# Decode attention with a gated MLP on one Trainium2 core: value products, queries and one projection take other places in the order of work

## The chip, the cores and the metric

The kernel runs on one core of one Trainium2 chip. The metric is device time in microseconds of one execution, the median of several runs. Beside the times there is one profiled execution, whose trace gives every instruction's start and duration and every DMA's issue.

## The reference, cut to what matters

Four sequences decode one token each. There are 32 heads of 128, a cache of 4096 keys and values per head, a model width of 512 and a gated MLP of 1792. All inputs are bf16.

```python
mod = (silu(c) @ w_mod).reshape(4, 6, 1, 512)          # sa, ca, ga, sb, cb, gb
h = layernorm(x) * (1 + ca) + sa
q = (h @ wq).reshape(4, 1, 32, 128)
p = softmax(q @ k_cache^T / sqrt(128))                 # 4 x 32 x 4096
x = x + ga * ((p @ v_cache).reshape(4, 1, 4096) @ wo)
h = layernorm(x) * (1 + cb) + sb
z = gelu(h @ w_in); z1, z2 = halves of z; z2 = layernorm(z2)
x = x + gb * ((z1 * (w_sp * z2 + b_sp)) @ w_out)
```

Keys and values are 134 MB each; all inputs together are 283 MB, and each byte is read once.

## The kernel before, in words

**Tiles.** The loop at L697 runs over 32 key tiles `i` of four heads each, 128 partitions by 128 key positions by 128 (4.2 MB). Tiles 0 to 23 come in pairs (`i` and `i + 1`): eight heads of one batch in one load of 8.4 MB. Tiles 24 to 31 are single. Keys alternate between the buffers bufA and bufB. Values use bufC, which a pair fills wholly and a single tile half; the values of tiles 30 and 31 go to bufB. `L` is 31.

**One tile.** VectorE multiplies the keys by the query in place, in two halves (`mult`, L391). TensorE sums the products over the head's width by matmuls with an identity (`reduce_d`, L399; 16 matmuls for a whole half, 4 for a quarter of one). VectorE sums what is left of that (`sum8`, L422), and three quarters of the second half by itself (`sum_rest`, L411). After a pair, or a single tile, `scores` takes the maxima (L435 to L452) and ScalarE the exponentials (`exps`, L465). `norm_r`, `norm_a` and `norm_b` (L479 to L502) sum them and invert. `pv` (L517) multiplies the exponentials by the values, 64 matmuls for a pair and 32 for a single tile; its result stands in `opss[0]` or `opss[1]` until `o_pick` (L526, L530), `o_cols` (L539, L542) and `o_scale` (L564, L570) have turned it into columns of the head outputs.

**Queries.** `queries(n)` for n from 0 to 7 does one batch and one half of the heads; with n = 0 and n = 4 come 16 matmuls with `wq` (L317), which lies in bufC. Each then spreads its rows by two or three matmuls into one PSUM tile (`qps`) that ScalarE copies out (L334, L335). `queries(0)` stands ahead of the loop, the others inside tile 0: two ahead of `mult(0, 1)`, five after `reduce_d(0, 1)`. `late_mod_a` (L352) and `late_mod_b` (L362 to L372, in tile 0) make the modulation of the later part.

**Output projection.** The heads of tiles 0 to 23 form three groups of eight. `deal(k)` (L636) and `dealt(k)` (L648, L654) bring a group's outputs into the layout of `wo`, and `project` (L666) multiplies all 24 heads in 24 matmuls; its result is copied out at L670. `turn` (L677, L681) adds the heads of tiles 24 to 27 and turns the rows into columns; `o_proj` (L611) does tiles 28 to 31. `add_up` (L688) adds the parts. Behind these come the second layer norm, the MLP (`gate`, L883; L908) and one product with `w_mod` (L916).

**Order.** Each engine works its instructions in the order in which the program issues them: the kernel switches to manual scheduling, and nothing is reordered. Semaphores order the engines among each other. All large loads are issued on SyncE's queue: `load_k`, `load_v`, `load_wo`, `load_end`. Each issue waits until its buffer is free, with all later ones behind it. In a pair's odd tile the value load is issued after the value product of the pair before, and at the tile's end the key load three tiles ahead.

**Where the value products stand.** In an odd tile `i` up to 23, `pv(i - 2)` follows `reduce_d(i, 0)`. For the later ones there are tables:

```python
PV_MID = {25: 23, 27: 24, 29: 26}     # after reduce_d(i, 0)
PV_END = {27: 25, 29: 27, 31: 28}     # at the end of tile i
```

`pv(29)` and `pv(30)` are called behind the loop.

**The end.** `deal(0)` and `deal(1)` run in tile 30, `deal(2)` and `deal(3)` at the end of tile 31; `dealt(0)` in tile 30, `dealt(1)` in tile 31 and the others behind the loop. There follow `project`, the steps of tile 28's output, `turn`, `pv(29)` with its steps, and `pv(30)` with its own.

Of the kernel before, what the change touches and what calls it, by code (L numbers as in the profile page):

```python
# [20 lines left out]
KIN = (slice(0, 2), slice(2, 4))  # L21
KG = (slice(0, 3), slice(3, 4))

PV_MID = {25: 23, 27: 24, 29: 26}
PV_END = {27: 25, 29: 27, 31: 28}
PICKS = {28: (24, 25), 30: (26, 27)}


# [25 lines left out]
def kernel(  # L54
# [16 lines left out]
    nc = tc.nc  # L71
    P = 128
    B, _, D = A_x.shape
# [83 lines left out]
    def load_v(i):  # L157
        if i < N0:
            load(bufC, kv_view(A_v_cache, i), (NP,))
        else:  # L160
            load(vts[i], kv_view(A_v_cache, i), TAIL if i == L else (NJ,))
# [148 lines left out]
    def queries(n):  # L310
        h, b = divmod(n, B)
        gs = slice(h * GQ, (h + 1) * GQ)
        if b == 0:
            qr = ps_sm([P, GQ, DH])
            for k in range(DJ):
                for q in range(HQ):
                    nc.tensor.matmul(  # L317
                        qr[R * q:R * (q + 1)], lhsT=hT[:, k, :], rhs=wq_v[:, k, gs, q, :],
                        start=(k == 0), stop=(k == DJ - 1), tile_position=(0, R * q),
                    )  # L320
            nc.scalar.copy(out=qrow[:, h], in_=qr)
        qp = ps_q().rearrange("p (g d) -> p g d", g=GQ)
        npair = 2 - h
        for k in range(2):
            nc.tensor.matmul(
                qp[:, 0:npair], lhsT=eb2[k][:, b].rearrange("p k q r -> p (k q r)"),
                rhs=qrow[:, h, k:2 * npair:2], start=(k == 0), stop=(k == 1),
            )
        if h:
            nc.tensor.matmul(  # L330
                qp[:, 2:4], lhsT=eb[:, b].rearrange("p q r -> p (q r)"), rhs=qrow[:, h, 2:4],
                start=True, stop=True,
            )
            nc.scalar.copy(out=qbo[:, :, b, :], in_=qp[:, 2:4])  # L334
        nc.scalar.copy(out=qbp[:, 2 * h:2 * h + npair, b, :], in_=qp[:, 0:npair])  # L335

    queries(0)

    sp_t = pre.tile([1, 2], BF16, name="sp_t")
    nc.scalar.dma_start(out=sp_t[:, 0:1], in_=B_w_sp[0:1, 0:1])  # L340
# [52 lines left out]
    def reduce_d(i, kc):  # L393
        ns = on_pe(i, kc)
        rd = 512 // ns
        kt = kts[i][:, kc * KC:kc * KC + ns, :]
        red = ps_red().rearrange("p (n r) -> p n r", r=rd)
        for m in range(DH // rd):
            nc.tensor.matmul(  # L399
                red, lhsT=ident_bf, rhs=kt[:, :, m * rd:(m + 1) * rd],  # L400
                start=(m == 0), stop=(m == DH // rd - 1),
            )
        st[i, "red", kc] = red
# [83 lines left out]
    def norm_a(i):  # L487
        if not pair(i):
            rsb = st.pop((i, "rsb"))
        elif i % (2 * B) == 2 * B - 1:  # L490
            rsb = st.pop(("P", i // 2 // B, "rsb")).rearrange("p b q h -> p (b q h)")
        else:
            return
        z = ps_sm(list(rsb.shape))
        nc.tensor.matmul(z, lhsT=inv_d, rhs=rsb, start=True, stop=True)  # L495
        st[i, "z"] = z
# [11 lines left out]
    def pv(i):  # L508
        n = (NP if pair(i) else NJ) // G
        pv_some(i, 0, n, n)  # L510
# [11 lines left out]
    def o_pick(i):  # L522
        ops = ops_of(i)
        sel = sels[HP if pair(i) else HQ]
        osb = wk.tile([P, DH], F32, name="osb", bufs=2)
        nc.vector.tensor_scalar(  # L526
            out=osb, in0=ops[:, 0, :], scalar1=sel[:, 0:1], scalar2=None, op0=ALU.mult
        )
        for g in range(1, G):
            nc.vector.scalar_tensor_tensor(  # L530
                out=osb, in0=ops[:, g, :], scalar=sel[:, g:g + 1], in1=osb,
                op0=ALU.mult, op1=ALU.add,
            )
        st[i, "osb"] = osb

    def o_cols(i):
        if pair(i):
            op = ps_sm([P, P])
            nc.tensor.transpose(op, st.pop((i, "osb")), ident_f)  # L539
        else:  # L540
            op = ps_sm([P, HQ])
            nc.tensor.matmul(op, lhsT=st.pop((i, "osb")), rhs=sel4, start=True, stop=True)  # L542
        st[i, "op"] = op
# [88 lines left out]
    def deal(k):  # L632
        n = HP if k < GP else HQ
        pp = ps_sm([P, n, B, n])
        for r in range(n):
            nc.tensor.matmul(  # L636
                pp[:, r], lhsT=picks[n][:, r, :],
                rhs=oTp[:, k * B:(k + 1) * B, :] if k < GP else oTs[:, 0:B, :], start=True, stop=True,
            )
        st["pp", k] = pp  # L640
# [3 lines left out]
    def dealt(k):  # L644
        pp = st.pop(("pp", k))
        n = pp.shape[1]
        ow = own if n == HP else own[:, 0:n * B, 0:n]
        nc.vector.tensor_tensor(  # L648
            out=ow, in0=pp.rearrange("p r b h -> p (r b) h"),
            in1=bc(mask8 if n == HP else mask4, n * B), op=ALU.mult,  # L650
        )
        od = late.tile([P, n, B], BF16, name=f"od{k}")
        with nc.allow_low_precision("all but one term of each sum are zero"):
            nc.vector.tensor_reduce(  # L654
                out=od.rearrange("p r b -> p (r b)"), in_=ow, axis=AX.X, op=ALU.add
            )
        st["od", k] = od
# [3 lines left out]
    def project():  # L661
        wp = ps_sm([B, D])
        for k in range(GP):
            od = st.pop(("od", k))
            for r in range(HP):
                nc.tensor.matmul(  # L666
                    wp, lhsT=od[:, r, :], rhs=wo_sb[:, k * HP + r, :],
                    start=(k == 0 and r == 0), stop=(k == GP - 1 and r == HP - 1),
                )
        nc.vector.tensor_copy(out=accR, in_=wp)  # L670

    def turn():
        od = st.pop(("od", GP))
# [19 lines left out]
        while adds:  # L693
            o_add(*adds.pop(0))

    QPLAN = {0: (1, 2, 3, 4, 5, 6, 7)}
    for i in range(NT):  # L697
        more = list(QPLAN.get(i, ()))
        mult(i, 0)
        if i >= 1:  # L700
            scores(i - 1)
        if i >= 2:
            norm_b(i - 2)
        todo = PICKS.get(i, (i - 3,) if i % 2 == 0 and 4 <= i <= N0 + 2 else ())
        reduce_d(i, 0)
        for t in todo:
            o_pick(t)
            o_cols(t)
        if i == 0:
            late_mod_b()  # L710
        if i == N0 + 2:
            nc.vector.memset(opss[1], 0.0)
        for k in range(2):
            if more:
                queries(more.pop(0))
        t = PV_MID.get(i, i - 2 if i % 2 and 3 <= i <= N0 else None)
        if t is not None:
            pv(t)
        if i == 1:
            load_v(1)  # L720
        elif i % 2 and i < N0:
            load_v(i)
        elif i == N0 + 1:
            load_v(N0)
            load_v(N0 + 1)
            nc.gpsimd.memset(pbd8, 0.0)
            nc.vector.memset(opss[0], 0.0)
            exps(N0)
        if i == L - 1:
            deal(0)  # L730
        mult(i, 1)
        if i >= 1:
            norm_r(i - 1)
        for t in todo:
            o_scale(t)
        sum8(i, 0)
        if i == L - 1:
            dealt(0)
        if i == L:
            dealt(1)  # L740
        reduce_d(i, 1)
        sum_rest(i)
        while more:
            queries(more.pop(0))
        if i >= 1:
            norm_a(i - 1)
        if i == L - 1:
            deal(1)
        if i == L:
            deal(2)  # L750
            deal(GP)
        if i in PV_END:
            if i == N0 + 3:
                load_v(N0 + 2)
            pv(PV_END[i])
        if i % 2 and i + 3 < N0:
            load_k(i + 3)
        elif i == N0 - 3 or i == N0 - 1 or i == N0 + 1:
            load_k(i + 3)
            load_k(i + 4)  # L760
        elif i == N0 + 3:
            load_v(N0 + 3)
            load_k(L - 1)
            load_k(L)
        elif i == L - 2:
            load_wo()
            late_consts()
            load_v(L - 3)
            load_v(L - 2)
        elif i == L - 1:  # L770
            load_v(L - 1)
        elif i == L:
            load_v(L)
            load_end()
# [10 lines left out]
    sbT = modT[:, DJ:2 * DJ, :]  # L785
    scores(L)
    norm_b(L - 1)
    for k in range(2, GP + 1):
        dealt(k)
    project()  # L790
    o_pick(L - 3)
    o_cols(L - 3)
    norm_r(L)
    norm_a(L)
    turn()
    o_scale(L - 3)
    norm_b(L)
    pv(L - 2)
    add_up()
    nc.vector.tensor_reduce(  # L800
        out=sel32, in_=ident_f.rearrange("p (q r) -> p r q", r=R), axis=AX.X, op=ALU.add
    )
    o_pick(L - 2)
    o_cols(L - 2)
    o_scale(L - 2)
    pv(L - 1)
    o_pick(L - 1)
    o_last(L, 0)
# [176 lines left out]
```

## Time and profile before

| | |
|---|---|
| median of 3 runs | 679.58 us (677.95 to 681.93) |
| profiled execution | 677.97 us; span of its instructions 676.2 us |
| VectorE (DVE) busy | 577.8 us, 85% |
| TensorE (PE) busy | 313.8 us, 46% |
| ScalarE (ACT) busy | 154.8 us, 23% |
| DMA | 283.09 MB, mean 419 GB/s, 97.3% of the span |
| mean granted TensorE clock | 0.745 |

The page divides the span into 40 slices of 16.9 us. Each digit of a row is the busy share of a slice in tenths. A row of the timeline has the start and the time in us, then engine, line, operation and tiles, and in brackets the idle time before it and what ended that. The chain of waits has start, us and what. In tables by stretch of time the columns after the stretch are its length and the busy us of PE, PE's weight loads, DVE, ACT and POOL, each with a count; then the clock, the DMA share and GB/s.

### The profile page before, as it was taken

What the parts mean: (1) busy time and instruction counts of PE and PEld (TensorE: products, weight loads), DVE (VectorE), ACT (ScalarE), POOL (GpSimd) and SP (SyncE); (2) the same over time, 40 slices, a digit from 0 to 9 for tenths busy, and PEclk for the clock granted to TensorE, in tenths of its full rate; (3) what the DMA queues carried; (4) which work ended last, traced back from release to release, by engine and by line L of the source; (5) the groups of instructions that cost most, each with busy time, mean ns of one, the idle gap of its engine ahead of it and who ended that gap; (6) DMA issues with size and microseconds to landing.
All of it is one profiled execution on the core that took longest, in us unless ns stands there. A gap on an engine that the chain in (4) does not pass through costs nothing.

```text
span 676.2 us, 5278 instructions
## 1 busy us (share of the span) xinstructions
PE 313.8 (46%) x2136; PEld 132.8 (20%) x2136; DVE 577.8 (85%) x437; ACT 154.8 (23%) x287; POOL 18.5 (3%) x55
## 2 busy tenths in 40 slices
PE   1374353633426354442436453342646325356876
PEld 0131121211112121110112121110212102122335
DVE  3266999989898998989898998989995999999624
ACT  1101606033050604114060503305061101111202
POOL 3000000000000000000000000000001000003000
PEclk9988777666778776666878766687877568787965
DMA  8999979999999999999999999999999999999991
GB/s 364 443 462 426 434 323 435 434 436 434 435 434 434 435 434 434 435 434 435 435 434 435 434 434 436 434 434 412 454 415 433 432 433 416 430 416 434 433 410 48
DMA packets 10222, 283.09 MB, mean 419 GB/s; under 512 B 972, under 2 KB 2900, under 8 KB 4052
## 3 DMA queue, kind: packets, MB, share of 16 engines
q1 hardware_dynamic: 10176, 282.73, 97.3%
q8 instruction: 17, 0.28, 0.1%
q14 instruction: 9, 0.07, 0.0%
q10 hardware_dynamic: 20, 0.01, 0.0%
HBM read 282.73 MB, written 0.00 MB: 418 GB/s over the span
## 4 chain that ended last, share of the span: by engine, by line
DVE 50%; DMA 34%; PE 13%; issue 1%; ACT 1%; POOL 0%; SPq 0%; DVEq 0%; ACTq 0%
DMA bB<-in_A_k_cache_dram 30%; DVE S L411 18%; DVE bB L391 17%; PE red L399 9%; DVE bA L391 6%; DMA bA<-in_A_k_cache_dram 4%; DVE S L422 3%; DVE osb L530 2%; PE ops L517 2%; PE sm L666 1%; DVE mrow L435 1%; DVE osb L526 1%; DVE mt L447 0%; DVE nM L449 0%; PE sm L225 0%
## 5 line engine op out<-in xcount | busy, mean ns | idle before, releaser
L465 ACT ACTIVATE pbd<-S,nb 32x256 bf16<-32x256 f32 x96 | 123.4, 1519 | 324.0 <-DVE nb L452 294.1
L399 PE MATMUL red<-bB,ident_bf 128*128 128x512 bf16 x344 | 108.7, 480 | 169.0 <-DVE bB L391 169.0
L399 PE MATMUL red<-bA,ident_bf 128*128 128x512 bf16 x332 | 110.1, 498 | 145.1 <-DVE bA L391 145.1
L399 PEld LDWEIGHTS <-ident_bf 128*128 128x128 bf16 x676 | 80.3, 121 | 447.9 <-issue 366.5
L391 DVE TENSOR_TENSOR bA<-bA,qbp 128x8192 bf16<-128x8192 bf16 x24 | 105.9, 4411 | 16.4 <-DMA bA<-in_A_k_cache_dram 16.4
L391 DVE TENSOR_TENSOR bB<-bB,qbp 128x8192 bf16<-128x8192 bf16 x24 | 106.0, 4417 | 9.6 <-DMA bB<-in_A_k_cache_dram 9.6
L411 DVE TENSOR_REDUCE S<-bA 128x48 f32<-128x6144 bf16 x15 | 98.1, 6543 | 0.0
L411 DVE TENSOR_REDUCE S<-bB 128x48 f32<-128x6144 bf16 x14 | 91.6, 6542 | 0.0
L422 DVE TENSOR_REDUCE S<-red 128x64 f32<-128x512 f32 x64 | 43.8, 684 | 15.6 <-PE red L399 15.4
L517 PE MATMUL ops<-bC,pbd 128*32 128x512 bf16 (+1 forms) x960 | 56.8, 388 | 0.0
L465 ACT ACTIVATION_READ_ACCUMULATOR pbd<-S,nb 32x1 f32 x96 | 46.9, 489 | 0.0
L465 ACT ACTIVATE pbd<-S,nM 32x128 bf16<-32x128 f32 x32 | 18.4, 576 | 119.1 <-DVE nM L449 80.3
L391 DVE TENSOR_TENSOR bA<-bA,qbo 128x8192 bf16<-128x8192 bf16 x8 | 35.3, 4410 | 0.0
L391 DVE TENSOR_TENSOR bB<-bB,qbo 128x8192 bf16<-128x8192 bf16 x8 | 35.3, 4409 | 0.0
L517 PEld LDWEIGHTS <-pbd 128*32 128x32 bf16 (+1 forms) x1008 | 25.4, 97 | 31.8 <-issue 9.7
L479 POOL TENSOR_TENSOR rsb<-maskd,rs 128x8 f32<-128x8 f32 x12 | 2.4, 202 | 493.8 <-ACT pbd L465 493.8
L530 DVE SCALAR_TENSOR_TENSOR osb<-ops,m,osb 128x128 f32<-128x128 f32 x36 | 12.6, 351 | 1.3
L495 PE MATMUL sm<-rsb,inv_d 128*128 128x4 f32 (+1 forms) x22 | 4.3, 273 | 15.8 <-POOL rsb L479 12.0
L530 DVE SCALAR_TENSOR_TENSOR osb<-ops,selg,osb 128x128 f32<-128x128 f32 x24 | 8.4, 351 | 0.8
L485 DVE TENSOR_SCALAR rsb<-maskd,rs 128x4 f32<-128x4 f32 x8 | 1.8, 222 | 7.3 <-ACT pbd L465 7.3
L495 PEld LDWEIGHTS sm<-rsb,inv_d 128*128 128x128 f32 x22 | 4.4, 223 | 18.6 <-POOL rsb L479 13.5
L465 ACT ACTIVATION_READ_ACCUMULATOR pbd<-S,nM 32x1 f32 x32 | 8.0, 250 | 0.0
(164 smaller groups left out, 156.8 us busy)
## 6 DMA issues: line engine op xcount, KB each, us to landing
bA<-in_A_k_cache_dram SPq DMA_DIRECT2D x6, 4096.0 KB, 37.3
bC<-in_A_v_cache_dram SPq DMA_DIRECT2D x6, 4096.0 KB, 22.0
bB<-in_A_k_cache_dram SPq DMA_DIRECT2D x3, 4096.0 KB, 32.3
bC<-in_A_wq_dram SPq DMA_DIRECT2D x1, 4096.0 KB, 12.3
bB<-in_A_k_cache_dram SPq DMA_DIRECT2D x2, 2048.0 KB, 36.8
bB<-in_A_v_cache_dram SPq DMA_DIRECT2D x1, 4096.0 KB, 18.5
bA<-in_A_wo_dram SPq DMA_DIRECT2D x3, 1024.0 KB, 29.6
bB<-in_A_v_cache_dram SPq DMA_DIRECT2D x3, 1024.0 KB, 16.6
```

Of the source, the lines that this page charges most:

```text
L391: nc.vector.tensor_tensor(out=kt, in0=kt, in1=bc(q, KC), op=ALU.mult)
L399: nc.tensor.matmul(red, lhsT=ident_bf, rhs=kt[:, :, m * rd:(m + 1) * rd], start=(m == 0), stop=(m == DH // rd - 1),)
L411: nc.vector.tensor_reduce(out=st[i, "S"][:, n0:NJ], in_=kts[i][:, n0:NJ, :], axis=AX.X, op=ALU.add)
L422: nc.vector.tensor_reduce(out=st[i, "S"][:, kc * KC:kc * KC + on_pe(i, kc)], in_=st.pop((i, "red", kc)), axis=AX.X, op=ALU.add,)
L435: nc.vector.tensor_reduce(out=mrow, in_=S, axis=AX.X, op=ALU.max)
L465: nc.scalar.activation(out=pbd8[r, :, 2 * q + h] if pair(i) else pbds[r, i % 4, :, q], in_=S[r, :], func=AF.Exp, bias=nM[r, h:h + 1], scal ...
L479: nc.gpsimd.tensor_tensor(out=st["P", g, "rsb"][:, b], in0=maskd[:, :, None].to_broadcast([P, HQ, 2]), in1=rs[:, None, :].to_broadcast([P, ...
L495: nc.tensor.matmul(z, lhsT=inv_d, rhs=rsb, start=True, stop=True)
L517: nc.tensor.matmul(ops_of(i)[g:g + rows], lhsT=pb[:, n, :], rhs=vt[:, n, :], start=(m < 4), stop=(m >= end - 4), tile_position=(0, g),)
L526: nc.vector.tensor_scalar(out=osb, in0=ops[:, 0, :], scalar1=sel[:, 0:1], scalar2=None, op0=ALU.mult)
L530: nc.vector.scalar_tensor_tensor(out=osb, in0=ops[:, g, :], scalar=sel[:, g:g + 1], in1=osb, op0=ALU.mult, op1=ALU.add,)
L666: nc.tensor.matmul(wp, lhsT=od[:, r, :], rhs=wo_sb[:, k * HP + r, :], start=(k == 0 and r == 0), stop=(k == GP - 1 and r == HP - 1),)
```

## The change

- All eight `queries` stand ahead of the loop, and so ahead of `late_mod_a` and of two small loads on ScalarE's queue (L340, L341).
- In odd tiles up to 23, `pv(i - 2)` and the value load after it stand ahead of `reduce_d(i, 0)`. `pv(24)` and `pv(26)` go to the same place in tiles 27 and 29. `pv(28)` moves from the end of tile 31 to its middle and `pv(29)` from behind the loop to the end of tile 31.
- `deal(2)` moves into tile 30. `dealt(1)` and `dealt(2)` stand in tile 31 ahead of `reduce_d(31, 0)`; `project` and `deal(3)` follow those sums; `rows_out` (the copy at L670), `dealt(3)` and `o_pick(28)` stand ahead of `reduce_d(31, 1)`. `o_cols(28)`, `turn` and `o_scale(28)` are at the end of tile 31. Behind the loop `add_up` and the steps of tile 29 are called ahead of the last `norm` steps, and `pv(30)` follows.

No instruction is added or removed, and each queue issues the same transfers in the same order.

```diff
--- before.py
+++ after.py
@@ -21,8 +21,9 @@
 KIN = (slice(0, 2), slice(2, 4))
 KG = (slice(0, 3), slice(3, 4))

-PV_MID = {25: 23, 27: 24, 29: 26}
-PV_END = {27: 25, 29: 27, 31: 28}
+PV_START = {27: 24, 29: 26}
+PV_MID = {25: 23, 31: 28}
+PV_END = {27: 25, 29: 27, 31: 29}
 PICKS = {28: (24, 25), 30: (26, 27)}


@@ -334,7 +335,8 @@
             nc.scalar.copy(out=qbo[:, :, b, :], in_=qp[:, 2:4])
         nc.scalar.copy(out=qbp[:, 2 * h:2 * h + npair, b, :], in_=qp[:, 0:npair])

-    queries(0)
+    for n in range(2 * B):
+        queries(n)

     sp_t = pre.tile([1, 2], BF16, name="sp_t")
     nc.scalar.dma_start(out=sp_t[:, 0:1], in_=B_w_sp[0:1, 0:1])
@@ -667,7 +669,10 @@
                     wp, lhsT=od[:, r, :], rhs=wo_sb[:, k * HP + r, :],
                     start=(k == 0 and r == 0), stop=(k == GP - 1 and r == HP - 1),
                 )
-        nc.vector.tensor_copy(out=accR, in_=wp)
+        st["rows"] = wp
+
+    def rows_out():
+        nc.vector.tensor_copy(out=accR, in_=st.pop("rows"))

     def turn():
         od = st.pop(("od", GP))
@@ -693,15 +698,21 @@
         while adds:
             o_add(*adds.pop(0))

-    QPLAN = {0: (1, 2, 3, 4, 5, 6, 7)}
     for i in range(NT):
-        more = list(QPLAN.get(i, ()))
         mult(i, 0)
         if i >= 1:
             scores(i - 1)
         if i >= 2:
             norm_b(i - 2)
         todo = PICKS.get(i, (i - 3,) if i % 2 == 0 and 4 <= i <= N0 + 2 else ())
+        t = PV_START.get(i, i - 2 if i % 2 and 3 <= i < N0 else None)
+        if t is not None:
+            pv(t)
+        if i % 2 and i < N0:
+            load_v(i)
+        if i == L:
+            dealt(1)
+            dealt(2)
         reduce_d(i, 0)
         for t in todo:
             o_pick(t)
@@ -710,17 +721,12 @@
             late_mod_b()
         if i == N0 + 2:
             nc.vector.memset(opss[1], 0.0)
-        for k in range(2):
-            if more:
-                queries(more.pop(0))
-        t = PV_MID.get(i, i - 2 if i % 2 and 3 <= i <= N0 else None)
-        if t is not None:
-            pv(t)
-        if i == 1:
-            load_v(1)
-        elif i % 2 and i < N0:
-            load_v(i)
-        elif i == N0 + 1:
+        if i == L:
+            project()
+            deal(GP)
+        if i in PV_MID:
+            pv(PV_MID[i])
+        if i == N0 + 1:
             load_v(N0)
             load_v(N0 + 1)
             nc.gpsimd.memset(pbd8, 0.0)
@@ -737,22 +743,25 @@
         if i == L - 1:
             dealt(0)
         if i == L:
-            dealt(1)
+            rows_out()
+            dealt(GP)
+            o_pick(L - 3)
         reduce_d(i, 1)
         sum_rest(i)
-        while more:
-            queries(more.pop(0))
         if i >= 1:
             norm_a(i - 1)
         if i == L - 1:
             deal(1)
+            deal(2)
         if i == L:
-            deal(2)
-            deal(GP)
+            o_cols(L - 3)
+            turn()
         if i in PV_END:
             if i == N0 + 3:
                 load_v(N0 + 2)
             pv(PV_END[i])
+        if i == L:
+            o_scale(L - 3)
         if i % 2 and i + 3 < N0:
             load_k(i + 3)
         elif i == N0 - 3 or i == N0 - 1 or i == N0 + 1:
@@ -785,24 +794,16 @@
     sbT = modT[:, DJ:2 * DJ, :]
     scores(L)
     norm_b(L - 1)
-    for k in range(2, GP + 1):
-        dealt(k)
-    project()
-    o_pick(L - 3)
-    o_cols(L - 3)
+    add_up()
+    o_pick(L - 2)
+    nc.vector.tensor_reduce(
+        out=sel32, in_=ident_f.rearrange("p (q r) -> p r q", r=R), axis=AX.X, op=ALU.add
+    )
+    o_cols(L - 2)
     norm_r(L)
     norm_a(L)
-    turn()
-    o_scale(L - 3)
+    o_scale(L - 2)
     norm_b(L)
-    pv(L - 2)
-    add_up()
-    nc.vector.tensor_reduce(
-        out=sel32, in_=ident_f.rearrange("p (q r) -> p r q", r=R), axis=AX.X, op=ALU.add
-    )
-    o_pick(L - 2)
-    o_cols(L - 2)
-    o_scale(L - 2)
     pv(L - 1)
     o_pick(L - 1)
     o_last(L, 0)

```

## The prediction

> **What bounds the kernel now.** I read the forty slices of the page first, then the transfers around the one weak slice, then the chain of waits, and last TensorE's order of time at the end. The page's DMA rows:
>
> ```profile
> DMA  8999979999999999999999999999999999999991
> GB/s 364 443 462 426 434 323 435 434 436 434 435 434 434 435 434 434 435 434 435 435 434 435 434 434 436 434 434 412 454 415 433 432 433 416 430 416 434 433 410 48
> ```
>
> The transfers run at about 434 GB/s from start to finish. There is one hole, in slice 6 (323 GB/s). Stretches of 8 us show its size (the last two columns are DMA share and GB/s):
>
> ```profile
> 88.00:96.00 8.00, 6.86 (x56) 2.80 (x59) 7.91 (x5) 0.00 (x0) 0.00 (x0) 0.76 0.93 401
> 96.00:104.00 8.00, 2.61 (x36) 1.00 (x29) 8.00 (x2) 0.00 (x0) 0.00 (x0) 0.88 0.70 264
> ```
>
> A share of 0.70 over 8 us leaves (1 - 0.70) x 8 = 2.4 us in which nothing moves. The DMA queue's order of time says why:
>
> ```profile
> 67.10 0.33 SPq L148 DMA_DIRECT2D bA<-in_A_k_cache_dram  x1
> 97.69 0.33 SPq L148 DMA_DIRECT2D bC<-in_A_v_cache_dram  x1
> ```
>
> Nothing was issued between these two. The values issued at 55.10 landed 23.7 us later, at 78.8; the keys issued at 67.10 are 8.39 MB, 19.3 us at 434 GB/s, so they are through at about 98, and the first DMA engines run dry before that. The values of tile 3 came too late, at 97.69, because they wait until the product of tile 1 (L517) has left bufC. The chain of waits shows what put that product there (start, us, what):
>
> ```profile
> 49.69 1.00 PE sm L317 x16
> ...
> 54.96 4.89 PE red L399 x16
> ...
> 60.49 6.54 DVE S L411
> ...
> 89.14 4.95 PE red L399 x16
> ```
>
> The queries stand inside key tile 0 and push the sums of tile 1 to 54.96. In tile 3 the product of tile 1 waits behind the sums at 89.14, and runs at 94.01 for 3.64 us.
>
> Later the chain changes hands. VectorE last waits for keys at 449.46 (issued 408.53, landing 40.93 later). From there to 634 its waits are these:
>
> ```profile
> DVE rsb L485 <- ACT pbd L465: 7.3, 1, 7.3
> DVE bB L391 <- DMA bB<-in_A_k_cache_dram: 1.4, 1, 1.4
> DVE S L422 <- PE red L399: 0.9, 1, 0.9
> ```
>
> So this stretch is VectorE's own work, save a stall of 7.3 us around tile 25 that both orders have. At 632 TensorE takes over (start, us, engine, line, operation):
>
> ```profile
> 632.78 3.61 PE L399 MATMUL red<-bB,ident_bf 128*128 128x512 bf16 x16 [2.39 <-DVE bB L391]
> ...
> 638.48 5.34 PE L666 MATMUL sm<-bA 128*4 128x512 bf16 x24
> ...
> 649.62 3.59 PE L517 MATMUL ops<-bC,pbd 128*16 128x512 bf16 x32
> ...
> 655.35 4.28 PE L517 MATMUL ops<-bB,pbd 128*16 128x512 bf16 x48
> ```
>
> TensorE is idle 2.4 us before the first line, and the projection of 24 heads stands alone on the path after it.
>
> **Part 1, queries ahead of the first keys.** Before, only batch 0's first group precedes the keys, and TensorE then idles 7.46 us until 33.42. Seven more `queries` calls go there. By the rows of tile 0 a first-half call repeats every 0.85 us (39.38, 40.23), a second-half call every 1.0 us (51.35, 52.36), and the second L317 group takes 1.05 to 1.90 us plus 0.7 for its copy. That is 3 x 0.85 + 2.6 + 4 x 1.0 = 9.2 us from 24.1, so to 33.3; `late_mod_a` (1.87 us) follows to 35.2. The first sums, due at 33.42, start some 1.7 us late, and `late_mod_b` and the second multiply of tile 0 with them. The two small loads on ScalarE's queue (L340, L341) move from 24.2 to about 33.6; `late_mod_b` needs them at about 41, their landing is in no view, and I put 0 to 1 us on it. Against that, tile 1's sums (54.96) no longer wait for 5.3 us of queries. Net, VectorE's multiply of tile 2 moves from 66.95 to about 63.2, with the key load issued beside it.
>
> **Part 2, value products ahead of the sums.** Tile 1's exponentials end 10.4 us after they start (73.41 to 83.8), so they end at about 80.1, and its values are in at 78.8. The product then takes 3.64 us, up to 7.2 at half clock (the 32-matmul product takes 1.90 us at 636.75 and 3.59 at 649.62). Tile 3's values are issued between 84 and 88 and not at 97.69, at least 8 us before the queue drains. The hole closes: **-2.4 us**. In the steady part this shift reaches the end, because VectorE takes each key pair as it lands (idle 2.18 and 2.53 us before the landings at 140.1 and 178.7), and every later landing moves with the queue.
>
> What it may cost: the product now blocks the sums, if its values are late. The page gives 24.6 us from issue to landing; 134.38 + 24.6 = 159.0, and tile 7's multiply runs 159.49 to 163.9. From 159.0 the product ends at 162.7 (full) or 166.2 (half), against 163.95 for the sums' start. A delay of up to 2.3 us meets VectorE's idle time of 1.4 to 2.5 us per pair. Only tile 23 (468.84) has no such idle time behind it. There the sums now end at 479.0; bounds are -0.85 us (the wait of 0.85 is gone, as TensorE is warm) and +3.6 us (half clock in both). I take 0: a product that starts 4 us earlier also brings the clock up earlier for the sums behind it.
>
> The Trainium skill speaks against this place: "TensorE: Matmul & The Clock Gate", Part 1, says that TensorE falls to half rate after about 3.4 us of idling and needs as long again to come back. By that rule each such product would begin cold, and tile 23 would be some 1 us later.
>
> The products of tiles 24 and 26 move the same way into VectorE's continuous stretch; TensorE is idle there, and their cost is nothing.
>
> **Part 3, the last key tile.** Both orders end the first multiply at 626.7. Afterwards TensorE has, back to back: sums 3.61, projection 5.2 (its three `od` are ready at 630.1, as two `dealt` of 0.87 us follow 628.34), `deal` 0.25, product of tile 28 1.85, sums 3.6, two small ones 0.4, `turn` 3.1 (646.54 to 649.62). That is 18.0 us, to 644.7; before, the product of tile 29 started at 649.62. VectorE's second multiply goes 1.8 us later, to 634.5, and is covered, since its sums start at 637.7. New waits in VectorE's order: `rows_out` for the projection (635.6) and `o_pick` for tile 28's product (637.7), with `dealt` and the last scores queued behind; both are done by 639.2, before the sums at 641.3. The last scores come 5.5 us later; ScalarE's exponentials end at 646.1, and they are needed at about 651.
>
> Then product of tile 29 (1.85 us at full clock, 3.55 at half), `o_pick` 1.5, `sel32` and the norm's small steps 1.0: tile 30's product starts at 649.1 or 650.8, not at 655.4. It too takes 1.85 instead of 3.45 if the clock holds. Gain: 655.4 - 649.1 + 1.6 = **7.9 us** at full clock, 655.4 - 650.8 = **4.6 us** at half. I take full clock: before, the granted clock held until 648.2, 4.4 us after the projection ended at 643.8, and now only 3.1 us of `turn` and then 2.5 us lie between dense groups.
>
> The remainder, 17.4 us from 658.8 to the end, is unchanged. Does data arrive for it? Moved by the full 10.3 us, the last value piece would be used at 654.2, and by its issue at 637.3 plus 16.4 us, less 2.4, it lands at 651.3; `gate` (658.3) needs weights landed by 656.5; L916 (661.4) needs 659.8. It is covered by 1.6 us at the narrowest.
>
> **Sum.** 676.2 - 2.4 - 7.9 = 665.9 span; the profiled execution took 677.97, 1.77 more than its span, so 667.7. The median shown, 679.58, is 1.6 above that execution. I forecast 668.5, between the two.
>
> **Rivals.**
> - *Cold end.* `turn` counts as idling, the clock drops, and both products run at half: 676.2 - 2.4 - 4.6 + 1.8 = 671.0. For it: 649.62 and 655.35 show exactly this. Against: TensorE is dense for 15 us just before. The page named above counts a whole idle window; by it this depends on where the window lies. Chance 0.22.
> - *One gain only.* Either the hole merely moves (a stall in tiles 0 to 3 beyond the 8 us of margin), or the end meets a new wait, late weights or a VectorE step waiting for TensorE: 677.97 - 2.4 = 675.6 at the worst, 670 at the best. Chance 0.12.
> - *No change.* Were the last transfers to bind the end, the gain could not pass the margins above; both gains would have to fail for 678 to 680. That the issue order on the DMA queue is untouched, and only its waits end earlier, speaks against. Chance 0.06.
> - *Slower, by the projection itself.* It now stands ahead of the last sums. With TensorE at half clock in 626 to 645, the dense work doubles: +13 us, and +3.3 for the two products: about 684. It decides once more than 60% of that work runs at half (10.3 of 16.3 us). Before, the clock was full from 624.3 to 648.2, which speaks against. Chance 0.08.
>
> **How the numbers follow.** My forecast has 0.52. From 665.0 (all terms at their best, with the 0.85 us) to 675.5 lie the forecast, the cold end with +3.6 us at tile 23, and most of the single gains. About half a per cent, 3.4 us, is what a measurement here can tell. Faster by more, below 676.2: 0.52 + 0.22 + 0.12 = 0.86; within: 0.06; slower: 0.08.
>
> **What would show it.** Right: no slice under 400 GB/s between 2 and 38; tile 3's values issued before 90; VectorE's keys of tile 22 landing at about 447; L666's group near 628, the product of tile 29 near 642.5, that of tile 30 near 647 at 1.9 us. Wrong: a TensorE wait for values longer than VectorE's idle time in the odd tiles, a granted clock of 0.5 between 624 and 642, or TensorE waiting for DMA after 650.

## The result, and the profile after

The changed kernel takes 668.59 us (median of 6 runs, 668.01 to 670.62) against 680.0 for the kernel before in the same comparison. The ratio is 0.984, with a 95% interval of 0.9817 to 0.9863. The forecast was 668.5. The profiled execution took 668.59 us, with a span of 666.8, 9.4 us under that of before. Most lines of code behind the first edit have higher numbers than before, by 1 to 11.

The page's DMA rows no longer have the hole:

```profile
DMA  8999999999999999999999999999999999999994
GB/s 362 452 441 413 440 437 437 433 441 441 436 436 429 418 436 440 433 429 434 436 440 433 436 426 429 441 440 410 440 440 420 436 426 429 439 419 433 437 413 167
```

The stretches of 8 us at that place, and the DMA queue's order of time:

```profile
88.00:96.00 8.00, 5.36 (x36) 2.03 (x28) 8.00 (x5) 0.00 (x0) 0.00 (x0) 1.00 1.16 502
96.00:104.00 8.00, 0.00 (x0) 0.10 (x1) 8.00 (x2) 0.00 (x0) 0.00 (x0) 0.59 0.95 411
```

```profile
66.40 0.33 SPq L149 DMA_DIRECT2D bA<-in_A_k_cache_dram  x1
88.82 0.33 SPq L149 DMA_DIRECT2D bC<-in_A_v_cache_dram  x1
```

Tile 3's values are issued at 88.82 and not at 97.69, so the queue still has about 9 us of keys to move; the share goes from 0.70 to 0.95. The keys of tile 22, which VectorE waited for until 449.46, now end its wait at 447.21. From there to 634 its waits of over 0.2 us are these:

```profile
DVE rsb L487 <- ACT pbd L467: 6.6, 1, 6.6
DVE bB L393 <- DMA bB<-in_A_k_cache_dram: 2.8, 1, 2.8
DVE osb L528 <- PE ops L519: 1.0, 1, 1.0
DVE qbp L675 <- PE sm L668: 0.5, 1, 0.5
```

TensorE's order of time at the end:

```profile
622.90 3.61 PE L401 MATMUL red<-bB,ident_bf 128*128 128x512 bf16 x16 [0.48 <-DVE bB L393]
626.44 5.34 PE L668 MATMUL sm<-bA 128*4 128x512 bf16 x24
...
633.74 3.63 PE L401 MATMUL red<-bB,ident_bf 128*128 128x512 bf16 x16
...
640.66 3.34 PE L519 MATMUL ops<-bC,pbd 128*16 128x512 bf16 x32
...
646.35 4.45 PE L519 MATMUL ops<-bB,pbd 128*16 128x512 bf16 x48
```

The first sums of tile 31 start at 622.90 instead of 626.78. From there TensorE works without a gap to tile 29's product at 640.66, where before it was at 649.62. From the start of these sums to the output's issue the kernel before took 47.1 us (626.78 to 673.92); the changed one takes 41.6 (622.90 to 664.54). So 3.9 us were gained ahead of tile 31 and 5.5 in it and behind it. VectorE's first wait for keys behind the hole, before and after, shows that 3.5 us had been gained there:

```profile
140.13 4.42 DVE L391 TENSOR_TENSOR bB<-bB,qbp 128x8192 bf16<-128x8192 bf16 x1 [2.18 <-DMA bB<-in_A_k_cache_dram]
136.65 4.42 DVE L393 TENSOR_TENSOR bB<-bB,qbp 128x8192 bf16<-128x8192 bf16 x1 [0.59 <-DMA bB<-in_A_k_cache_dram]
```

### The profile page after: what moved, and what is told of

It reads as the page before. It is cut to its first block, busy times and chain, and to the rows that moved or that the text cites. A ratio compares the mean times of both kernels' runs of the same rounds, so it can differ in the third digit from the quotient of the medians.

```text
span 666.8 us, 5276 instructions
## 1 busy us (share of the span) xinstructions
PE 315.9 (47%) x2136; PEld 137.1 (21%) x2136; DVE 577.0 (87%) x437; ACT 154.9 (23%) x287; POOL 18.5 (3%) x55
## 4 chain that ended last, share of the span: by engine, by line
DMA 46%; DVE 35%; PE 15%; ACT 3%; issue 1%; POOL 0%; SPq 0%; DVEq 0%; ACTq 0%
DMA bC<-in_A_v_cache_dram 29%; DMA bB<-in_A_k_cache_dram 12%; DVE S L413 12%; DVE bB L393 10%; PE ops L519 8%; DVE bA L393 6%; PE red L401 3%; DMA bC<-in_w_mod_dram 3%; DVE S L424 2%; ACT pbd L467 2%; DVE osb L532 2%; DMA bC<-in_B_b_sp_dram 1%; PE sm L668 1%; PE qps L326 1%; PE sm L318 1%
## 5 line engine op out<-in xcount | busy, mean ns | idle before, releaser
L401 PE MATMUL red<-bB,ident_bf 128*128 128x512 bf16 x344 | 97.9, 443 | 123.8 <-DVE bB L393 123.8
L401 PE MATMUL red<-bA,ident_bf 128*128 128x512 bf16 x332 | 96.7, 451 | 124.4 <-DVE bA L393 124.4
L401 PEld LDWEIGHTS <-ident_bf 128*128 128x128 bf16 x676 | 74.3, 111 | 364.7 <-issue 232.4
L519 PE MATMUL ops<-bC,pbd 128*32 128x512 bf16 (+1 forms) x960 | 79.7, 502 | 54.8 <-DMA bC<-in_A_v_cache_dram 49.7
L519 PEld LDWEIGHTS <-pbd 128*32 128x32 bf16 (+1 forms) x1008 | 34.1, 119 | 99.8 <-issue 50.0
L528 DVE TENSOR_SCALAR osb<-ops,selg 128x128 f32<-128x128 f32 x8 | 2.7, 340 | 6.8 <-PE ops L519 6.8
```

What stands on the lines that cost most here:

```text
L401: nc.tensor.matmul(red, lhsT=ident_bf, rhs=kt[:, :, m * rd:(m + 1) * rd], start=(m == 0), stop=(m == DH // rd - 1),)
L519: nc.tensor.matmul(ops_of(i)[g:g + rows], lhsT=pb[:, n, :], rhs=vt[:, n, :], start=(m < 4), stop=(m >= end - 4), tile_position=(0, g),)
L528: nc.vector.tensor_scalar(out=osb, in0=ops[:, 0, :], scalar1=sel[:, 0:1], scalar2=None, op0=ALU.mult)
```

## The experiments

Each time is a median beside runs of the kernel before on the same chip: 679.22 us for the first four, 679.99 for the next four, 679.92 for the last three. Brackets behind a ratio hold its 95% interval.

**Queries back.** `e1_queries_back` undoes part 1 alone.

```diff
-    for n in range(2 * B):
-        queries(n)
+    queries(0)
...
+    QPLAN = {0: (1, 2, 3, 4, 5, 6, 7)}
```

> The changed kernel with the queries back inside key tile 0, as before; the value products and the last tile stay changed. Theory A (the hole at 96 us is closed by the value product's place alone, the queries bring nothing): the exponentials of tile 1 end at 83.8 as before, the product runs from there to about 89.4, tile 3's values are issued near 89.6, ahead of the queue's end at 98, so no hole: 668.6 us, within 0.7. Theory B (my prediction's reading, the queries' shift is needed for part of it): tile 3's values are issued after 94 and part of the 2.3 us returns, 670 to 671.

Measured: 669.79 us, ratio 0.9852 [0.983, 0.9875]. The time lies between the two expectations and decides nothing: the interval overlaps that of the changed kernel. The trace does decide on the hole. Tile 3's values are issued at 88.94, against 88.82 with the queries ahead, and the two stretches at 88 to 104 move 426 and 443 GB/s. The hole needs no queries to close. The traced execution took 671.64 us, 1.9 above the median.

**The end alone.** `e2_end_only` is the kernel before with part 3.

```diff
-PV_MID = {25: 23, 27: 24, 29: 26}
-PV_END = {27: 25, 29: 27, 31: 28}
...
+PV_MID = {25: 23, 27: 24, 29: 26, 31: 28}
+PV_END = {27: 25, 29: 27, 31: 29}
...
+        if i == L:
+            project()
+            deal(GP)
...
```

> The kernel before with the last key tile's change alone (project, deal, dealt, turn, products of tiles 28 and 29). Theory A (the traces' arithmetic: from the end of tile 31's first multiply to tile 30's output pick the changed kernel is 5.6 us shorter): 680.0 - 5.6 = 674.4, between 673.5 and 675.5. Rival (the end's gain is only there because the earlier part moved the transfers forward, or the reverse, the rest of 3.8 us depends on it): over 677 or under 672.

Measured: 673.41 us, ratio 0.9919 [0.9896, 0.9942], a gain of 5.8 us; 0.1 below the range given, and neither rival's. In its trace the hole is there:

```profile
96.00:104.00 8.00, 3.53 (x52) 1.48 (x45) 8.00 (x2) 0.00 (x0) 0.00 (x0) 1.00 0.73 281
```

From the first sums of tile 31 (628.85) to the output's issue (670.75) it takes 41.9 us, against 41.6 in the changed kernel. The gain at the end stands by itself. This kernel and `e1_queries_back` differ in nothing but the early value products, and ran in the same comparison: 673.41 and 669.79. So the early products are worth 3.6 us there.

**Tile 3's product alone.** `e3_tile3_only` keeps the changed kernel's place for one early value product and returns the others.

```diff
-PV_START = {27: 24, 29: 26}
-PV_MID = {25: 23, 31: 28}
+PV_START = {}
+PV_MID = {25: 23, 27: 24, 29: 26, 31: 28}
...
-        t = PV_START.get(i, i - 2 if i % 2 and 3 <= i < N0 else None)
-        if t is not None:
-            pv(t)
-        if i % 2 and i < N0:
-            load_v(i)
+        if i == 3:
+            pv(1)
+            load_v(3)
...
```

> The changed kernel, but of the value products only that of tile 1, in tile 3, stands ahead of the sums; those of tiles 3 to 21, 24 and 26 are back behind them. Theory A (one product closes the hole; of the others only the one in tile 23 matters, where VectorE's wait of 0.85 us for the sums comes back): hole closed, keys of tile 22 still land near 447.2, 668.6 + 0.9 = 669.5, between 668.8 and 670.3. Rival B (all the early issues are needed to keep the DMA queue full): a new hole, 670.5 or more. Rival C (no other product matters): 668.6.

Measured: 669.74 us, ratio 0.986 [0.9837, 0.9882], in Theory A's range. The hole is closed (87.93 for the issue; 427 GB/s at 96 to 104). Theory A's reason for the missing 0.9 us is not in the trace: VectorE has no wait for the sums of tile 23, though the product stands behind them. Nor do the keys of tile 22 land near 447.2, as expected, but at 448.48: 1.3 us later than in the changed kernel, after the same first landing behind the hole (136.65 in both). Why is open. So one of the products closes the hole, and for the others no effect is shown.

**Queries alone.** `e4_queries_only` is the kernel before with part 1.

```diff
-    queries(0)
+    for n in range(2 * B):
+        queries(n)
...
-    QPLAN = {0: (1, 2, 3, 4, 5, 6, 7)}
+    QPLAN = {}
```

> The kernel before with all eight query groups ahead of the loop and nothing else. Theory A (VectorE's tile 2 starts only 0.7 us earlier, 66.25 and not 66.95, so tile 3's values are issued near 97.0 and the hole shrinks by at most 0.7 us): 679.3 to 680.0. Rival (the queries inside tile 0 cost several us at the end): 677.5 or less.

Measured: 679.51 us, ratio 0.9999 [0.9986, 1.0013]: no difference, Theory A's time. Its mechanism was not quite met in the profiled execution (676.96, 2.5 us under the median): tile 3's values were issued at 95.47, most of the hole was closed (393 and 396 GB/s), and the keys of tile 22 landed at 447.19, as early as in the changed kernel. So in this execution the queries alone nearly closed the hole; the median of 679.51 has no gain from it, and there is no trace of an execution near the median.

**Tile 23's product first.** `e5_v23_first` moves the one product that the change left behind the sums.

```diff
-PV_START = {27: 24, 29: 26}
-PV_MID = {25: 23, 31: 28}
+PV_START = {25: 23, 27: 24, 29: 26}
+PV_MID = {31: 28}
```

> The changed kernel, with the value product of tile 23 also ahead of the sums, in tile 25 (the one product that the change left behind them). VectorE waits 6.6 us there for exponentials that wait for a memset that waits for this product. Theory A (the wait goes, and then the transfers bind the end): the last weights land at 658.9 and are used at 662.3, the output weights land at 657.5 and are used at 661.6, so only 3.4 us of the 6.6 can be kept: 668.6 - 3.4 = 665.2, between 664.5 and 666.2. Rival B (the transfers do not bind): 662.0. Rival C (VectorE's wait only moves to another place): 668.0 to 669.

Measured: 664.79 us, ratio 0.9782 [0.9763, 0.9801]: Theory A. VectorE's wait in tile 25 falls from 6.6 to 0.9 us, and the first sums of tile 31 start at 618.05, 4.9 us earlier. TensorE's waits from 615 on show where the rest stops:

```profile
PE ops L519 <- DMA bB<-in_A_v_cache_dram: 2.1, 2, 1.1
...
PE qps L555 <- DMA bB<-in_A_v_cache_dram: 0.6, 1, 0.6
```

None of these is in the changed kernel. The products now wait for the values of tiles 30 and 31, and of 4.9 us the span keeps 3.9 (666.8 to 662.9). The waits are for values, where the expectation named the weights. They cost more than the 1.0 us that is missing: in this trace tile 29's product happened to take 1.90 us and not 3.34, and that made up for part of the 2.7 us of waits.

**End products beside dense work.** `e6_end_products` puts tile 29's product ahead of `turn` and tile 30's straight behind it. `o_pick` of tile 29 moves ahead of `add_up`.

```diff
-PV_END = {27: 25, 29: 27, 31: 29}
+PV_END = {27: 25, 29: 27, 31: 30}
...
         if i == L:
+            pv(L - 2)
             o_cols(L - 3)
             turn()
...
```

> The changed kernel, with tile 29's value product straight after the last sums and ahead of turn, and tile 30's straight after turn, so that both follow dense work. Theory A (the two products run at half clock because turn stands ahead of them; moved, tile 29's takes 1.9 us and not 3.3, tile 30's starts near 642.8 and not 646.4, and the transfers bind at 3.4 us): 665.2, between 664.6 and 667.0. Rival B (the clock drops in the same free-running window anyway): tile 29's product still takes over 3 us and the gain is 1 us or less, 667.6 to 668.6.

Measured: 666.42 us, ratio 0.9801 [0.9781, 0.9821], in Theory A's range, but not at its 665.2. Its lines of TensorE:

```profile
638.41 1.90 PE L519 MATMUL ops<-bC,pbd 128*16 128x512 bf16 x32
...
643.59 3.38 PE L519 MATMUL ops<-bB,pbd 128*16 128x512 bf16 x32
```

Straight behind the sums 32 matmuls take 1.90 us, at a granted clock of 1.00 (full speed); 32 of the same size behind `turn` take 3.38, at 0.55. The clock is the cause of the difference. The end, from the first sums of tile 31 to the output's issue, takes 38.9 us and not 41.6. In this trace 1.0 us of that is lost ahead of it, mostly since the sums of tile 30 took 6.34 us and not 4.98. TensorE has no wait for values at the end: the transfers did not bind here.

**Both.** `e7_both` joins the two edits before.

> Both edits of the two kernels before together. Theory A (transfers bind the end after either): no more than either alone, 664.5 to 666. Rival B (the gains add): 661 or less.

Measured: 664.8 us, ratio 0.9782 [0.9762, 0.9801]. The gains do not add: TensorE waits 2.7 us for tile 30's values (its product starts at 640.94, and behind the wait it takes 3.59 us), and Theory A stands.

**Small loads first.** `e8_small_loads_first` issues the loads of `B_w_sp` and `B_b_sp` ahead of the queries.

```diff
-    for n in range(2 * B):
-        queries(n)
-
     sp_t = pre.tile([1, 2], BF16, name="sp_t")
     nc.scalar.dma_start(out=sp_t[:, 0:1], in_=B_w_sp[0:1, 0:1])
     nc.scalar.dma_start(out=sp_t[:, 1:2], in_=B_b_sp.rearrange("(a b) -> a b", b=1))
+    for n in range(2 * B):
+        queries(n)
```

> The changed kernel, with the two small loads on ScalarE's queue ahead of the query groups and not behind them. In the changed kernel the second was issued at 34.6 and landed at 43.0, and VectorE's second multiply of tile 0 started at 43.7. Theory A (that wait costs VectorE about 2 us in tile 0, and nothing at the end, since the queue has 7 us of stock when tile 3's values are issued at 88.8): multiply of tile 0 near 41.8, values of tile 3 near 87, time 668.6 within 0.7. Rival B (the lost 2 us reach the end): 666.6.

Measured: 668.56 us, ratio 0.9834 [0.9815, 0.9852]; VectorE's second multiply of tile 0 starts at 41.86 and not at 43.71, tile 3's values are issued at 85.41. The first keys behind the hole are taken at 136.65, as in the changed kernel, and those of tile 22 at 446.95 and not at 447.21. So once the queue does not run dry, a still earlier issue brings almost nothing. The traced execution took 670.73 us, 2.2 above the median.

**Both kernels again.** `e9_before_again` and `e10_after_again` are the two kernels unchanged, traced a second time.

> The kernel before, unchanged, for a second trace of it beside the changed one on the same chip. The two traces so far explain 2.25 us (hole) and 5.5 us (end); 1.65 us more lie in tiles 23 and 25, where the granted clock fell otherwise. Theory A (those two are chance of the clock): in this trace the wait for sums in tile 23 and the exponentials' wait in tile 25 differ from 0.85 and 7.32 by up to 1 us either way. Theory B (they belong to the order of work): they come again within 0.2 us. Hole again 2 to 3 us; time 679 to 680.

> The changed kernel, unchanged, for a second trace. Theory A (chance of the clock): tile 25's wait differs from 6.63 us by up to 1 us, and tile 29's product from 3.34 us; no hole; 668 to 670. Theory B (order of work): 6.6 and no wait for sums in tile 23 again.

Measured: 679.45 us, ratio 0.9998 [0.9983, 1.0012], and 670.1 us, ratio 0.9859 [0.9844, 0.9874]. The hole came again (share 0.71, issue at 98.95) and was again closed. Tile 29's product took 3.42 us. Tile 25's wait is 7.3 us in both, so the 0.7 us by which it differed in the first pair was chance of the clock: Theory A. In all four traces this wait is 1.15 to 1.17 us longer than tile 25's sums, and these go with the clock: 5.46 us of sums at a granted clock of 0.65 in the first trace after, 6.12 to 6.17 us at 0.58 in the other three.

Tile 23 fits Theory B in these four traces: a wait for sums of 0.85 and 0.89 us before, none after. The other traces say that the clock decides there as well. With the product behind, the wait grows with the time of the sums: none at 4.98 us (`e3_tile3_only`, clock 0.72), 0.85 at 5.70 (before, 0.63), 1.67 at 6.52 (`e2_end_only`, 0.55). With the product ahead it is gone while the product takes 5.8 us or less, and is 0.71 and 0.98 us where that took 6.5 (`e1_queries_back` and `e8_small_loads_first`).

In the second pair 4.8 us were gained ahead of tile 31 (first sums at 628.24 and 623.47) and 6.3 from there to the output's issue (675.41 and 664.32). Of these 11.1 us the spans show 9.8: in the second trace after, the time from the output's issue to the end of the span is 3.6 us, against 2.3 in the second trace before.

**Tile 23's product first, queries back.** `e11_v23_first_queries_back` joins the edit of `e5_v23_first` and that of `e1_queries_back`.

> The changed kernel with tile 23's value product ahead of the sums in tile 25, and with the queries back inside tile 0. Theory A (the queries' place brings nothing, and the transfers bind the end): 664.8 within 0.7, as with the queries ahead. Theory B (the queries' place is worth the 1.2 us by which the kernel with queries back was above the changed one): 666.0.

Measured: 665.77 us, ratio 0.9799 [0.9781, 0.9817], between the two. The interval overlaps that of `e5_v23_first`. Both comparisons of the queries' place, this one and `e1_queries_back`, put it at about 1 us the same way, each within its interval. So an effect of about 1 us is neither shown nor excluded, and no trace shows where it would lie.

## Why the prediction was right, point by point

The time came out as forecast, and two of its terms did not: they made up for each other. The two places of the gain were right; that the sum came out to 0.1 us is luck.

- **The hole: right in the place and the cause, the size in part by luck.** It was put at 2.4 us and at one product, that of tile 1. Tile 3's values were forecast between 84 and 88 and came at 88.8. The first keys behind the hole came 3.5 us earlier in the first pair of traces and 5.2 in the second (141.65 and 136.49). The keys of tile 22 came 2.25 us earlier in the first pair and 3.8 in the second (450.89 and 447.06). So the prediction's step that every later landing moves with the queue did not quite hold: 1.2 to 1.3 us were lost on the way, and no run shows why.
- **The queries: right that they cost nothing at the end, wrong on the way.** The multiply of tile 2 was to start at 63.2 and started at 66.25. The term that was mis-sized is the 0 to 1 us for the small loads. The chain of waits after has the wait for the second of them:

```profile
34.58 8.45 DMA bC<-in_B_b_sp_dram
```

- It landed 8.45 us after its issue, at 43.0, when `late_mod_b` was due at about 41. `e8_small_loads_first` takes this wait away: there the multiply of tile 2 starts at 63.35, as forecast, and the time stays.
- **The products ahead of late values: right.** TensorE's waits after (sum, number, longest) have the price of the place:

```profile
PE ops L519 <- DMA bC<-in_A_v_cache_dram: 49.7, 10, 6.7
```

VectorE's waits after have hardly any of it:

```profile
DVE S L424 <- PE red L401: 2.2, 3, 1.2
```

- Ten products stand up to 6.7 us waiting for their values, but mostly in time in which TensorE had nothing else. VectorE's waits for sums fell from 15.4 us (12 times) to 2.2 (3 times).
- The prediction named a wait for values longer than VectorE's idle time (1.4 to 2.5 us) as a sign of being wrong. Such waits came, and did no harm: the sign should have been the time at which the product ends, against that at which the sums behind it can start.
- The two products that start at 427.94 and 466.53, each behind a wait of 6.06 us, take 5.61 and 5.09 us and not 3.64, at granted clocks of 0.64 and 0.70. The sums behind them take 3.63 us at 1.00, where before those of tile 23 took 5.7: the product brings the clock up for them, as the prediction took. This agrees with the Trainium skill ("TensorE: Matmul & The Clock Gate", Part 1), which says that TensorE drops to half rate after an idle window of about 3.4 us.
- Tile 23 did not come some 1 us later, as the prediction said it would by that rule. VectorE waits there in two of the eight traces with the product ahead, by at most 0.98 us; before, it waits 0.85.
- **The end: the mechanism right, the size 2.4 us too large.** The step that failed is "I take full clock". Tile 29's product took 3.34 us, at a granted clock of 0.56, and tile 30's 2.9. So the gain was 5.5 and not 7.9: this is the rival that the prediction called the cold end, for which it had 4.6. Dense work ended at 637.3, and 3.4 us of small matmuls, those of `turn` above all, stood between. The granted clock fell at about 640.2, ahead of the product. The prediction's reason was that it had held for 4.4 us behind the projection before; here it held for 2.9. `e6_end_products` shows that the place matters. It is not all: in `e5_v23_first` the product behind the same `turn` took 1.90 us, at 1.00. What decides between the two cases is open.
- **What made up for it.** 3.9 us were gained ahead of tile 31, where the sum had 2.4. In the first pair 0.95 us of that lies in tile 23 and 0.7 in tile 25 (VectorE's wait 7.3 before, 6.6 after). The second pair shows the latter to be chance. The bound of -0.85 that the prediction gave for tile 23 was reached; there too the clock decides, and with the product ahead it cost VectorE less.
- **Transfers at the end: right.** They were to cover the end by 1.6 us at the narrowest, with the larger gain, and TensorE has no wait for a transfer from 615 on. `e5_v23_first` and `e7_both`, which are faster, ran into the values of tiles 30 and 31.

Between the two kernels the medians differ by 11.4 us in the first comparison and by 9.4 to 9.8 in the second; the end alone is worth 5.8 us (`e2_end_only`), and the early products on top of it 3.6 (`e1_queries_back` against it). These 9.4 us cover the second difference; the 2 us that the first has on top are not in its traces, whose spans differ by 9.4.

## What to carry to other kernels

Where transfers run at a steady rate, look for the one stretch below it, and ask which instruction held the issue back and what stood ahead of that on its in-order engine; one value product in one tile was enough here. Work that waits for late data may stand ahead of other work if the engine has nothing else ready until then: compare the landing and the next input's time in that tile. After each gain, check against the landings of the last transfers: here the next 4.9 us brought 2.7 us of new waits for values.

## What was not expected of the hardware

- A load of two bytes took 8.45 us from issue to landing (7.0 in `e4_queries_only`), issued on another queue while large loads were moving (441 GB/s in that slice of the page).
- `turn`'s matmuls of four columns did not always hold the granted clock. They follow dense work without a gap and last some 3 us; tile 29's product behind them took 2.98 to 3.51 us in seven traces and 1.90 in one (`e5_v23_first`), with the same order at this place.
- Sums of the same 16 matmuls in tile 25 took between 5.37 us (granted clock 0.67) and 6.57 us (0.54) over the traces in which no value product stood ahead of them. Time multiplied by clock gives 3.5 to 3.6 us for both: the clock explains the difference.
